# A new order of work on all engines for a linear-attention and gated feed-forward layer

## The chip, the core and the metric

The kernel runs on one core of one Trainium2 chip. The metric is the device time of one execution in microseconds (us). Five engines work side by side, each through its own queue of instructions and in the order of that queue: PE (TensorE, matrix multiplication), DVE (VectorE), ACT (ScalarE), POOL (GpSimd) and SP (SyncE, which here only starts transfers). They wait for one another by semaphores. PE writes into PSUM, which has 8 banks; a matmul group needs a bank that nobody reads any more.

## What is computed

One layer on 2048 tokens of width 448, in bf16: linear attention with softmax features, and a gated feed-forward part, each behind a layer normalisation and with a residual.

```python
q, k, v = split(layernorm(x) @ wqkv)          # 16 heads of 28
pq, pk = q @ w_phi, k @ w_phi                  # per head
phi_q = concat(softmax(pq), softmax(-pq))      # the same for phi_k
kv = einsum("bhsf,bhsd->bhfd", phi_k, v);  z = sum_s phi_k
o = einsum("bhqf,bhfd->bhqd", phi_q, kv) / (einsum("bhqf,bhf->bhq", phi_q, z) + 1e-6)
h = x + o @ wo
y = layernorm(h)
out = h + (sigmoid(y @ w_gate) * (y @ w_up)) @ w_down     # inner width 1792
```

## The kernel before

The tokens are cut into 16 tiles of 128. Keys and values come first: all 16 tiles have to go into `kv` before any output of the attention can be made. The query side follows, and then the feed-forward part in five blocks of 2, 2, 4, 4 and 4 tiles. The query work of the later tiles lies between the matmuls of the first two blocks.

For each tile `t` the query side goes through these tasks:

- `qp`: PE multiplies the normalised tokens with the folded query weights (L516, `Wq,xT`).
- `eqp`, `eqm`: ACT takes the exponentials of plus and minus the result (L653, tile `eq`). The buffer `eq` has 12 places, so tile `t` can be written only when the transpose of tile `t - 12` has read it: tile 13 waits for `eT` 1.
- `hs`: POOL adds halves (L667, `halves`); `sq`: DVE sums (L670); `rq0` on DVE and `rq` on POOL (L674) form the ratio of the two softmax sums.
- `em`: POOL, or DVE by choice, scales the minus half by it (L680, `eq<-eq,rq`).
- `eT`: SP starts a transposing transfer `eqT<-eq` (L688), one tile each for tiles 0 to 3, and two tiles each for 4, 6, 8, 10, 12, 14.
- `num`: PE multiplies with the sums `kvz` (L708, eight matmuls a tile); `rd` and `o` on DVE divide (L716 `rden`, L718 `o_pad`).
- `oT`: a transfer transposes the output of two tiles (L739), and `wo_` (L516, `wo_sb,oT`) projects it.
- `h` adds the residual (L773 on DVE, L759 on ACT for the first tiles); `bst2`, `agg2` (DVE, L776, L778), `ve2`, `pow2`, `nb` (POOL, L779, L781, L792) and `hn` (ACT L794, DVE L796) normalise; `hT` transposes the normalised tokens (for tiles 0 and 1 by PE and a copy, L809 on ACT or L812 on DVE; for the others by a transfer of two tiles, L815, `xT<-hn`).

For each block the feed-forward part runs `gu` on PE (L516, `xT` with `wg_sb` and `wu_sb`, two banks each), `tg` on ACT (L851, tanh), `hh` on DVE (L858), `dn` on PE (L877, `wd_sb,hh`), `fin` on DVE (L884) and `st`, the store (L886). `hh` frees the two banks of its `gu`; `o` frees the bank of its `num`; `fin` that of its `dn`. In the text `gu` 0 is the first of these matmul groups, `num` 10 that of tile 10, and so on. `dm` (L821) are spare matmuls that fill PE's time early in the program and compute nothing.

The order on all engines is written out: `PLAN` (from L30) is a string of task numbers. A suffix `.4-4` names the PSUM banks, and `~` puts a task on its other engine. `planned()` takes the tasks in that order and adds to each what it must wait for (what it reads, and whoever last used its banks); `emit()` then gives every engine its queue:

```python
        for item in PLAN.split():
            if item[-1] == "~":
                t = self.list[int(item[:-1])]
                t.eng, t.fn = t.alt[0], t.alt[2]
```

The durations and landings that stand in the task definitions do not take part in this; they are for whatever makes the string. A transposing transfer gets one of 12 semaphores in turn, a store one of 8.

Of the kernel before, what the change touches and what calls it, by code (L numbers as in the profile page):

```python
# [35 lines left out]
124 123 35 206 210 216 209 36 37 217 686.2-2 687.0-0 688.0-0 689.0-0 690.0-0 684.0-0 691.0-0 692.0-0 693.0-0 150
189.0-2 202 148 207.1-5 190 200 193 38 208 218 211 219 149 212 220 89.3-3 93.4-4 85.6-6 81.2-2 94 82 86 146 196 90
223.0-7 95 144 91 96 92 151 145 147 87 203 83 84 88 221 152 153 39 40 161 159 213 125 126 214 241.1-5 224 234 197.4-4
204 118.6-6 109.2-2 119 154 110 160 155 120~ 157 235 41 242 228 237 225.3-7 111 156 245 246 45 112.6-6 113 115.2-2 116
215 117 114 158 222 226 229 236 227 238 239 46 47 261.1-2 48 162 248 166 163 243.3-6 49 164 262 253 249 170 230  # L40
331.0-7 252 250 265 244 167 165 231 272 255 332 254 259.1-2 232 333 168 334 277.5-6 256 172 247 260 335 257 340
279.0-3 339 169 171 173 263 278 336 174 341 264 337 280 175 271 347.1-7 266 282 338 281 233 342 240 267 251 270 343
283~ 345 268 348 290 284 313.0-2 357 289 295.3-5 176 285 344 273 288 314 356 286 346 296 291 324 297.6-7 325 274 306
50 292 258 275 327 269 307 51 298 318 52 315.2-5 309 317 53 293 308 54 276 328 287 310 299 55 316 320 300 433.0-7 319
311 302 326 294 399.2-3 301 321 303 349 434 322~ 350 382.5-6 443 304~ 400 442 383 435 329~ 402 305 312 323 409 330 358
401 365.1-7 467 468 408 351 359 469.4-4 392 436 474.3-3 470 391 528.2-2 366 360 471 361 362 475 472.4-4 416.0-6 352
368 476 473 364 353 367 385 384 477.3-3 354 529 478~ 355 532.1-1 530 533 369 363 374 550 531 417 551 534 552 375
450.3-5 556 418 553 557 535~ 425 558 554.7-7 451 559 370 555 426 560.1-1 376 482.7-7 419 561~ 479.2-2 460 371 735.0-1
480 483 372 459 728.4-6 484 373 453 737 481 727.5-7 730 452 386 377 485 739 729 733 740 743.2-3 393 731 734 736.0-1 56
387 745 378 738 732 379 752.4-6 380~ 741 767.5-7 747 742 381 754 388 769 748 389 536.0-1 394 757 390 758 776.2-3 395  # L50
771 537 396 772 397 751.4-6 569 778 410 398 562 753 744.1-5 570 781 755 759.0-7 403 756 746 571 782 760.4-6 749 411
761 762 750 427 775.2-3 563 765 768.1-5 763 412 564 766 777 565 764 572 770 573 566 779 496.0-0 773 780 489.7-7 567
493.4-4 774 486.2-2 497 783.1-1 490 487 574 491 575 404 568 428 420 494 576 495 444 786.7-7 421 405 784 406 437 422
488 407 429 445 492 438 498 797.1-2 413 461 806.4-5 799 439 787 499 805.0-3 423 801 414 808 802 790.6-7 811 430
789.1-2 415 431 812 792 446 791 795 798.4-5 440 793 454 796 807 794 800 462 540.1-2 447 803 424 809 804 814.6-7 810
541 455 816 463 599 456 448 441 821.0-3 819 538.4-5 449 600 592 823 539 825 601 820 602 813.1-2 826 457 432 458 577
584 829.6-7 815 822.0-4 603 817 585 831 604 824 818 464 833 830.3-5 578 605 465 837.1-2 834 827 832 593 838.6-7 466
785 835 586 594 839 828 587 595 840 579 836 596 841 514.0-0 843 842 500.4-4 503.3-3 588 844 510.1-1 597 501 507.2-2
589 598 845.6-6 502 580 581 504 606 505 582 583 511 512 590 506 515 517.1-1 846 848.3-3 591 508 509 518 513 521.2-2
849 524.6-6 542.4-7 522 525 516 852.3-5 519 526 543 523 859.0-1 520 614 854 615 868.2-7 857 607 861 858 544.4-6 616  # L60
608 863 867.3-5 864 545 870 527 629 869 622 630 546.0-6 871 623 873 883.1-4 631 874 547 609 624 872 851.2-7 610 632
611 885 612 637 644 633 613 548.0-3 638 634 887 617 888 645 853 618 625 876.5-6 626 855 619 856 892.1-4 627 620~ 549
635~ 628 900.2-7 652 646 659 894 636 621 647 639 653 891.0-3 897 660 788 878 654 661 847 898 655 648 881 662 640 893
902 649 882 663 860.1-4 641 895 875.5-6 642 896 656 643 862 657 905 664 658~ 927.0-3 865 650 866 877 929 665~ 906
936.1-4 931 666 879 932 919.2-7 880 651 938 921 951.5-6 923 924 941 884.0-3 942 953 886 928.1-4 889 955 899.2-7 956
930 890 901 933 935.0-3 920.5-6 934 903 904 960.2-7 943.1-4 962 922 965 937 966 925 945 926 944.2-7 947 939 948
987.5-6 940 959.1-4 946 961 949 952.0-3 950 989 963 954 964 957 967.2-7 991 958 968.1-4 969 970 910.0-0 973 913.3-3
971 911 974 972 981.2-2 907.7-7 908 982 914 983 850 916.1-1 992 917 988.2-3 996.5-6 909 912 990 1003.1-7 1011.0-4 993
994 1005 998 1012.2-3 1001 1007 1002 1013 1008 1014 995.5-6 1017 1015 1016 1018 1027.1-7 997 1036.0-4 999 1000 1029
1038 1031 1004.5-6 1032 1041 1042 1035.2-3 1006 1037 1019.0-4 1009 1020.1-7 1021 1010 1023 1028.5-6 1024 1022 1030  # L70
1025 1053.0-0 1026 1033 1034 1039 1049.4-4 1040 978.1-1 1057.2-2 1046.3-3 1054 1058 1043.5-5 1050 1044 1059 975.5-5
1055 1051 979 1052 980 1045 915 984.1-1 976 1056 1047 1048 1060 977 1061.3-3 985 918 1062 986 1063 1064
"""


# [851 lines left out]
```

## Time and profile before

| | |
|---|---|
| median of three runs | 203.79 us (203.53, 203.79, 204.76) |
| profiled execution, its own time | 203.44 us |
| its span (first to last instruction) | 201.7 us |
| granted TensorE clock | 1.00 |
| PE busy | 195.5 us, 97% |
| DVE, ACT, POOL busy | 134.4, 93.5, 75.7 us |
| longest wait of PE | 2.2 us at L708, for a transpose of query features |

The profile is one execution. Its page gives the busy time of each engine, the chain of waits followed back from the last instruction, and the costliest groups. In a list of waits, `PE ps L708 <- DMA eqT<-eq: 2.2, 1, 2.2` says that PE, before the instruction of line 708, waited for a transfer from `eq` to `eqT`, 2.2 us in total, once, 2.2 at the longest. In a timeline a row has its start, its length, the engine, the line, the operation and the tiles, and how many instructions are joined in it (x4).

### The profile page before, as it was taken

How to read it: one execution, taken by the hardware profiler on the slowest of the kernel's cores; microseconds unless marked ns; L12 is line 12 of the kernel's file. 1: busy time of each engine (PE TensorE's matmuls, PEld its weight loads, DVE VectorE, ACT ScalarE, POOL GpSimd, SP SyncE). 2: the span in 40 equal slices, each digit the busy share in tenths (PEclk: the TensorE clock that was granted, in tenths of full speed). 3: DMA queues.
4: the chain of work that ended last, by engine and by line, in shares of the span. 5: the costliest groups of instructions: out<-in, count | busy, mean ns of one | idle time of the engine just before them, and what ended most of it. 6: DMA issues, size and time to landing. Idle time of an engine off the chain costs nothing.

```text
span 201.7 us, 4990 instructions
## 1 busy us (share of the span) xinstructions
PE 195.5 (97%) x2051; PEld 109.6 (54%) x2051; DVE 134.4 (67%) x315; ACT 93.5 (46%) x179; POOL 75.7 (38%) x130
## 2 busy tenths in 40 slices
PE   8999999999989999978999999999999999999995
PEld 5655545555488858864544444444445444445553
DVE  3999999998899997994779866345411425432052
ACT  2977999999974424263022455424420015330000
POOL 6339799956676789771003560000000000000000
PEclk9999999999999999999999999999999999999999
DMA  5899981699828628599422062200000110000024
GB/s 138 211 248 219 213 297 38 112 395 365 136 54 128 130 55 183 101 163 215 97 52 52 4 149 54 57 0 3 0 0 2 50 44 0 3 0 0 3 79 126
DMA packets 49543, 21.06 MB, mean 104 GB/s; under 512 B 40304, under 2 KB 48496, under 8 KB 49520
## 3 DMA queue, kind: packets, MB, share of 16 engines
q1 hardware_dynamic: 49376, 20.71, 43.8%
q8 instruction: 16, 0.26, 0.6%
q14 instruction: 7, 0.06, 0.1%
q10 hardware_dynamic: 144, 0.03, 0.1%
HBM read 9.20 MB, written 1.84 MB: 55 GB/s over the span
## 4 chain that ended last, share of the span: by engine, by line
PE 90%; DVE 4%; DMA 3%; POOL 1%; issue 1%; ACT 0%; SPq 0%
PE ps L516 57%; PE ps L877 21%; DMA eqT<-eq 3%; PE ps L631 2%; PE ps L821 2%; PE ps L708 2%; PE ps L427 1%; PE ps L445 1%; PE ps L477 1%; PE ps L587 1%; DVE x_sb L773 1%; POOL rs L781 1%; DVE sq L670 1%; DVE hn L788 0%; PE ps L753 0%
## 5 line engine op out<-in xcount | busy, mean ns | idle before, releaser
L516 PE MATMUL ps<-xT,wg_sb 64*128 64x512 bf16 (+1 forms) x490 | 87.6, 333 | 0.6 <-DVE rden L716 0.6
L516 PE MATMUL ps<-xT,wu_sb 64*128 64x512 bf16 (+1 forms) x490 | 87.6, 333 | 0.0
L851 ACT ACTIVATE tg<-ps 128x512 f32<-128x512 f32 (+1 forms) x70 | 34.2, 512 | 75.4 <-PE ps L516 70.1
L858 DVE SCALAR_TENSOR_TENSOR hh<-tg,ps 128x512 bf16<-128x512 f32 (+1 forms) x70 | 39.0, 573 | 30.5 <-ACT tg L851 29.1
L516 PEld LDWEIGHTS ps<-xT,wg_sb 64*128 64x128 bf16 x490 | 45.5, 94 | 21.9 <-issue 1.4
L516 PEld LDWEIGHTS ps<-xT,wu_sb 64*128 64x128 bf16 x490 | 45.5, 94 | 15.4
L877 PE MATMUL ps<-wd_sb,hh 128*128 128x448 bf16 (+2 forms) x252 | 43.3, 332 | 0.0
L877 PEld LDWEIGHTS ps<-wd_sb,hh 128*128 128x128 bf16 x252 | 23.0, 98 | 19.3 <-issue 0.8
L884 DVE SCALAR_TENSOR_TENSOR x_sb<-ps,x_sb 128x448 bf16<-128x448 f32 (+2 forms) x18 | 9.5, 562 | 26.4 <-PE ps L877 26.3
L653 ACT ACTIVATE eq<-ps,rs 128x448 bf16<-128x448 f32 x32 | 18.2, 731 | 0.0
L667 POOL TENSOR_TENSOR halves<-eq 128x448 f32<-128x448 bf16 x14 | 13.4, 971 | 5.7 <-DVE eqT L621 3.3
L680 POOL TENSOR_TENSOR eq<-eq,rq 128x448 bf16<-128x448 bf16 x15 | 14.0, 940 | 0.6
L516 PE MATMUL ps<-Wq,xT 64*128 64x448 bf16 x112 | 12.5, 350 | 0.0
L516 PE MATMUL ps<-Wvc,xT 64*128 64x448 bf16 x112 | 12.4, 350 | 0.0
L516 PE MATMUL ps<-wo_sb,oT 64*128 64x448 bf16 x98 | 11.7, 349 | 0.0
L779 POOL TENSOR_SCALAR rs<-mv 128x1 f32<-128x1 f32 x14 | 2.7, 191 | 23.1 <-DVE mv L778 22.3
L794 ACT ACTIVATE hn<-x_sb,nb,rs 128x512 bf16<-128x512 bf16 x10 | 7.9, 808 | 6.9 <-POOL nb L792 6.9
L516 PE MATMUL ps<-Wk,xT 64*128 64x448 bf16 x98 | 10.7, 350 | 0.0
L601 ACT ACTIVATE hh<-ps,rs 128x448 bf16<-128x448 f32 x16 | 9.6, 677 | 0.4 <-PE ps L587 0.3
L601 ACT ACTIVATE eqT<-ps,rs 128x448 bf16<-128x448 f32 x16 | 9.8, 686 | 0.0
L718 DVE TENSOR_TENSOR o_pad<-ps,rden 128x448 bf16<-128x448 f32 x16 | 9.4, 608 | 0.2
L535 DVE BATCH_NORM_STATS2 st<-x_sb 128x6 f32<-128x448 bf16 x16 | 9.4, 599 | 0.0
(118 smaller groups left out, 219.8 us busy)
## 6 DMA issues: line engine op xcount, KB each, us to landing
wg_sb<-in_B_w_gate_dram SPq DMA_DIRECT2D x2, 896.0 KB, 7.0
wu_sb<-in_B_w_up_dram SPq DMA_DIRECT2D x2, 896.0 KB, 7.9
out_dram<-x_sb SPq DMA_DIRECT2D x14, 112.0 KB, 1.8
x_sb<-in_A_x_dram SPq DMA_DIRECT2D x3, 448.0 KB, 4.5
wd_sb<-in_B_w_down_dram SPq DMA_DIRECT2D x3, 448.0 KB, 11.8
hh<-in_A_wqkv_dram SPq DMA_DIRECT2D x4, 196.0 KB, 3.6
wo_sb<-in_A_wo_dram SPq DMA_DIRECT2D x2, 336.0 KB, 4.4
hh<-in_A_wqkv_dram SPq DMA_DIRECT2D x2, 224.0 KB, 3.4
```

Source lines behind the costliest of these rows:

```text
L516: r = e.matmul(ap(), lhsT=st(blk, rows), rhs=mv(blk, rows), start=first and i == 0, stop=not first and i == 2, tile_position=(rows.start, 0))
L535: task(("bst", t), "dve", 0.53, lambda e, t=t: e.bn_stats(st1[:, t % 4, :], X(t)), [x_ld[t], opt(("agg", t - 4))])
L601: task((key, t), "act", 0.53, lambda e, t=t, s=s, i=i, b=kb: e.activation(signs(ek[s])[:, :, :, i, :], heads2(bank[b()][:, 0:D]), ACT.Exp, ...
L653: task((key, t), "act", 0.53, lambda e, w=w, t=t, i=i, b=bk[j]: e.activation(signs4(eq[:, w, :, 0:GP])[:, :, :, i, :], heads2(bank[b()][:, ...
L667: task(("hs", t), "pool", 0.9, lambda e, w=w, half_=half_, by4=by4: e.tensor_tensor(half_, by4(eq[:, w, :, 0:GP])[:, :, :, 0:DH // 2], by4 ...
L680: return e.tensor_tensor(ap, ap, rq[:, w, :].rearrange("p (k h) -> p k h", h=2)[:, :, :, None].to_broadcast([P, NPAIR, 2, DH]), ALU.mult)
L718: task(("o", t), "dve", 0.56, lambda e, t=t, res=res: e.tensor_tensor(o_pad[:, t % 4, 64 * (t % 2):64 * (t % 2) + D].rearrange("p (h d) -> ...
L794: task(("hn", t), "act", 0.56, lambda e, t=t, hnv=hnv: e.activation(hnv(), windows(X(t)), ACT.Identity, bias=nb[:, t:t + 1], scale=rs2[:, ...
L851: task(("tg", c, f_), "act", 0.51 if n == 4 else 0.3, lambda e, j=j, N=N, b=gb[i]: e.activation(tg[:, j % NSG, 0:N], bank[b()][:, 0:N], AC ...
L858: e.scalar_tensor_tensor(hhT[c % 2][:, f_, 0:N], tg[:, j % NSG, 0:N], 1.0, bank[b()][:, 0:N], op0=ALU.add, op1=ALU.mult), deps)
L877: r = e.matmul(bank[b][:, cols], lhsT=hhT[c % 2][:, f_, ts], rhs=wd_sb[:, f_, cols], start=(f_ == 0), stop=(f_ == FT - 1))
L884: e.scalar_tensor_tensor(X(t)[:, cols], bank[got(first)[0]][:, cols], 0.5, X(t)[:, cols], op0=ALU.mult, op1=ALU.add), [nm, ("hn", t)])
```

## The change

Only the string `PLAN` differs: the order of the tasks on all engines, their banks, and which tasks run on their other engine. It was searched with longer planned landings for the transposes `eT`, `oT` and `hT`. No task, shape or buffer is changed. There are 28 filler matmuls instead of 27. `em` 5 goes from DVE to POOL, the residual `h` 1 and the copy `hT` 1 from DVE to ACT, `hT` 0 from ACT to DVE, and `hn` 4 and `hn` 5 from ACT to DVE.

```diff
 PLAN = """
-18 0 20 16 21 57.7-7 42 22 7 1 58 13 59 8 60 9 6 4 680.0-0 44 14 23 5 24 15 10 25 61 26 11 62 19 12 17 667.0-0 73.0-0
...
+13 10 0 16 18 11 17 21 57.7-7 42 5 3 9 19 4 6 43 20 14 58 2 22 59 7 1 12 15 23 8 60 24 25 61 26 27 28 29 62 667.0-0
...
 """
```

POOL, in the stretch in which the query features of tiles 8 to 15 are scaled; `halves` is `hs`, `rq` is `rq`, `eq<-eq,rq` is `em`. Before, the tiles are in this order: `rq` 9, `hs` 15, `rq` 10, `em` 9, `rq` 11, `em` 11, `rq` 12, `hs` 14, `rq` 13, `em` 10, 13, 12.

```order
L674 TENSOR_TENSOR rq<-rq,sq 128x16
L667 TENSOR_TENSOR halves<-eq 128x448
L674 TENSOR_TENSOR rq<-rq,sq 128x16
L680 TENSOR_TENSOR eq<-eq,rq 128x8x2x28
L674 TENSOR_TENSOR rq<-rq,sq 128x16
L680 TENSOR_TENSOR eq<-eq,rq 128x8x2x28
L674 TENSOR_TENSOR rq<-rq,sq 128x16
L667 TENSOR_TENSOR halves<-eq 128x448
L674 TENSOR_TENSOR rq<-rq,sq 128x16
L680 TENSOR_TENSOR eq<-eq,rq 128x8x2x28 x3
L779 TENSOR_SCALAR rs<-mv 128x1
```

After, the same stretch: `rq` 13, `hs` 14, `rq` 12, `em` 13, `hs` 15, `em` 12, `rq` 15, 10, 14, 11, `em` 10, 11, 15, 14.

```order
L674 TENSOR_TENSOR rq<-rq,sq 128x16
L667 TENSOR_TENSOR halves<-eq 128x448
L674 TENSOR_TENSOR rq<-rq,sq 128x16
L680 TENSOR_TENSOR eq<-eq,rq 128x8x2x28
L667 TENSOR_TENSOR halves<-eq 128x448
L680 TENSOR_TENSOR eq<-eq,rq 128x8x2x28
L674 TENSOR_TENSOR rq<-rq,sq 128x16 x4
L680 TENSOR_TENSOR eq<-eq,rq 128x8x2x28 x4
L779 TENSOR_SCALAR rs<-mv 128x1 x2
```

`em` 13 and 12 moved ahead of `em` 10 and 11. SP's queue has `eT` 8, 12, 10, 14 in this order in both.

PE at the end of the second block. Before, `num` 12, 8, 9, 11, 10, then `dn` 2, `num` 13, `dn` 3, `num` 14, 15, and the output projection `wo_` of tile 4:

```order
L708 MATMUL ps<-kvz,eqT 128x58 x40
L877 MATMUL ps<-wd_sb,hh 128x448 x14
L708 MATMUL ps<-kvz,eqT 128x58 x8
L877 MATMUL ps<-wd_sb,hh 128x448 x14
L708 MATMUL ps<-kvz,eqT 128x58 x16
L516 MATMUL ps<-wo_sb,oT 128x448 x8
L516 MATMUL ps<-xT,wg_sb 128x512
```

After, `num` 10, 13, 12, 9, 11, 8, then `dn` 3 and `dn` 2, `num` 15, 14, and the first `gu` of the third block:

```order
L708 MATMUL ps<-kvz,eqT 128x58 x48
L877 MATMUL ps<-wd_sb,hh 128x448 x28
L708 MATMUL ps<-kvz,eqT 128x58 x16
L516 MATMUL ps<-xT,wg_sb 128x512
L516 MATMUL ps<-xT,wu_sb 128x512
```

All six `num` moved ahead of both `dn`, and a `gu` pair ahead of `wo_`.

SP around the first transposes of query features, before (`eT` 0 and 1, then the second halves of the gate and up weights):

```order
L359 DMA wg_sb<-in_B_w_gate_dram 128x2x1792
L688 DMA_TRANSPOSE eqT<-eq 128x8x128 x2
L359 DMA wu_sb<-in_B_w_up_dram 128x2x1792
L359 DMA wg_sb<-in_B_w_gate_dram 128x2x1792
L359 DMA wu_sb<-in_B_w_up_dram 128x2x1792
```

After:

```order
L359 DMA wg_sb<-in_B_w_gate_dram 128x2x1792
L359 DMA wu_sb<-in_B_w_up_dram 128x2x1792
L688 DMA_TRANSPOSE eqT<-eq 128x8x128
L359 DMA wg_sb<-in_B_w_gate_dram 128x2x1792
L359 DMA wu_sb<-in_B_w_up_dram 128x2x1792
L688 DMA_TRANSPOSE eqT<-eq 128x8x128
```

One weight load moved ahead of `eT` 0, and the two after it ahead of `eT` 1.

More of the change, by code (lines that the diff above doesn't have):

```diff
@@ L36 @@
[L36 to L65, printed above, removed]
@@ new lines @@
+497 495 437 498 407 438 499 446 784 447 454 422 439 797.0-7 415 790.1-3 787 799 440 448 792 801 798.4-5 795 802
+806.2-6 461 796 789.0-7 455 808 441 456 791 462 811 793 449 463 812 464 540.1-3 800 429 423 794 541 457 430 424 803
+805.0-7 599 821.2-6 592 431 807 823 804 809 538.1-3 600 825 465 432 593 829.4-5 458 826 539 810 814.2-6 594 601 584
+595 813.0-7 602 596 577 816 831 466 603 597 585 819 815 820 830.1-3 817 586 822.2-6 833 587 818 604 598 832 578
+837.0-7 835 834 824 838.4-5 827 579 839 605 580 828 836 606 785 840 581 841 507.2-2 517.1-1 582 843 842 514.3-3 588
```

47 lines of the change are left out of this document (36 added, 11 removed).

## The prediction

> **What bounds the kernel now.** I read the page first, then the waits of the matmul engine, then the chain, then the timelines around the one long wait. The page:
>
> ```profile
> span 201.7 us, 4990 instructions
> PE 195.5 (97%) x2051; PEld 109.6 (54%) x2051; DVE 134.4 (67%) x315; ACT 93.5 (46%) x179; POOL 75.7 (38%) x130
> PE 90%; DVE 4%; DMA 3%; POOL 1%; issue 1%; ACT 0%; SPq 0%
> PEclk9999999999999999999999999999999999999999
> ```
>
> PE is busy 195.5 of 201.7 us at full granted clock, and 90% of the chain is PE's own work. The change takes no matmul of the computation away, so all it can win is PE's idle time, 6.2 us, and at most what is filler. The waits that PE shows, engine first, then what was waited for, total, times, longest:
>
> ```profile
> PE ps L708 <- DMA eqT<-eq: 2.2, 1, 2.2
> PE ps L516 <- DVE rden L716: 0.6, 1, 0.6
> ```
>
> One wait matters: 2.2 us, once, for a transpose of query features (`eT`, L688) ahead of `num` (L708). The 0.6 comes at 56 us, at the first feed-forward matmul. The chain through the long wait (start, duration, work):
>
> ```profile
> 84.31 0.36 SPq L688
> 84.72 6.86 DMA eqT<-eq
> 91.58 0.14 issue
> 91.72 0.61 PE ps L708 x16
> 92.33 2.65 PE ps L877 x14
> ```
>
> The transpose issued at 84.72 landed 6.86 us later, and PE had run dry before it:
>
> ```profile
> 88.71 0.85 PE L708 MATMUL ps<-kvz,eqT 112*128 112x58 bf16 x24
> 91.72 0.61 PE L708 MATMUL ps<-kvz,eqT 112*128 112x58 bf16 x16 [2.15 <-DMA eqT<-eq]
> 94.82 0.39 PE L708 MATMUL ps<-kvz,eqT 112*128 112x58 bf16 x8
> 98.25 0.93 PE L516 MATMUL ps<-wo_sb,oT 64*128 64x448 bf16 x8
> ```
>
> Three `num` (8, 9, 12; eight matmuls each) run at 88.71, and `num` 11 and 10 start at 91.72. From there to the end PE hardly waits: it is busy 51.00 of 51.00 and 31.00 of 31.00 us in the next stretches, so what is won here reaches the end.
>
> ```profile
> 99.00:150.00 51.00, 51.00 (x470) 23.26 (x467) 29.70 (x58) 19.35 (x33) 7.81 (x24) 1.00 0.16 37
> 150.00:181.00 31.00, 31.00 (x248) 14.57 (x247) 11.76 (x19) 6.67 (x12) 0.00 (x0) 1.00 0.05 16
> ```
>
> (Columns: window, length, PE, PEld, DVE, ACT, POOL busy, clock, DMA share, GB/s.)
>
> **Why that transpose was late, and what the change moves.** SP's queue holds `eT` 8, 12, 10, 14 in this order in both kernels, each for two tiles. What fed them is on POOL and SP:
>
> ```profile
> 69.75 0.50 POOL L792 TENSOR_SCALAR nb<-mv,rs 128x1 f32<-128x1 f32 x2
> 71.36 1.90 POOL L667 TENSOR_TENSOR halves<-eq 128x448 f32<-128x448 bf16 x2 [1.10 <-DVE sq L670]
> 77.51 0.22 POOL L674 TENSOR_TENSOR rq<-rq,sq 128x16 f32<-128x16 f32 x1
> 77.81 0.94 POOL L680 TENSOR_TENSOR eq<-eq,rq 128x448 bf16<-128x448 bf16 x1
> 80.00 2.74 POOL L680 TENSOR_TENSOR eq<-eq,rq 128x448 bf16<-128x448 bf16 x3
> 82.77 1.90 SPq L688 DMA_TRANSPOSE eqT<-eq  x1
> 84.72 6.24 SPq L688 DMA_TRANSPOSE eqT<-eq  x2
> ```
>
> POOL scales tile 11 at 77.81 (`em`, L680), then 10, 13, 12 in the three from 80.00 to 82.74. So the transposes of 12 and 10 are both released by the last one: 12 issues at 82.77 for 1.90 us, and 10 stands behind it until 84.72, although its data were ready at 80.9 (80.00 and a third of 2.74). The new order puts `em` 13 and 12 ahead of 10 and 11, which suits the queue.
>
> *POOL.* From `hs` 13 to the end of `em` 12 there are now five `hs`, four `rq`, four `em`; then four `rq`, and `em` 10, 11. A `halves` costs 0.93 to 0.97, half of the 1.90 row; an `em` 0.91, a third of 2.74; an `rq` 0.2. That is 5 x 0.95 + 4 x 0.2 + 4 x 0.91 = 9.2 us, and 4 x 0.2 + 2 x 0.91 = 2.6 more. Start: at best 70.25, directly behind the `nb` row, at worst 71.36, if the 1.10 us wait for DVE stays. `em` 12 then ends at 79.4 to 80.6 (82.74 before), `em` 11 at 82.0 to 83.2. I take the early end, since the first `halves` is another tile's now and needs another `sq`.
>
> *The transposes.* `eT` 12 issues at 79.4 and is through SP by 81.3; `eT` 10 issues at 82.0 instead of 84.72. Landing after issue, over all ten (min, median, max):
>
> ```profile
> L688 SPq DMA_TRANSPOSE eqT<-eq x10: 1232/1802/3547, 33.4 to 87.4; - x10
> DMA to landing us min/median/max: 3.1/4.3/6.9
> ```
>
> `eT` 10 so lands at 86.3 by the median and at 88.9 by the maximum; from the late start, 87.5 to 90.1. PE comes to these `num` at about 88.7, as before. The wait of 2.15 goes but for 0.2 at the bad ends; taken: all of it.
>
> *What is late next there.* PE now runs all six `num` (x48) ahead of both down-projections (`dn` 3, `dn` 2, L877). They take 1.4 us, to 90.1 (0.23 each: two `num` start at 91.72, and the next work, of 2.65, starts that much before 94.82, at 92.17). `dn` 3 also needs the last `hh` of the block:
>
> ```profile
> 88.47 1.25 DVE L858 SCALAR_TENSOR_TENSOR hh<-tg,ps 128x256 bf16<-128x256 f32 x3
> 89.64 0.25 DVE L716 RECIPROCAL rden<-ps 128x16 f32<-128x16 f32 x1
> 89.92 0.62 DVE L718 TENSOR_TENSOR o_pad<-ps,rden 128x448 bf16<-128x448 f32 x1
> ```
>
> It ended at 89.72, and in the new order one `rden` (0.25) is put before it: 90.0, beside the 90.1. So `dn` starts at 90.1 with six `num` done, against 92.17 with five done. Gain 92.17 + 0.23 - 90.1 = 2.3. `hn` 5 and 4 come from ACT to DVE behind that, and six divisions of 0.82 follow beside the 5.3 us of the two `dn`; the first of them frees the bank that the next `num` needs, so they are hidden, unless `hn` waits over 4 us for POOL.
>
> *56 us.* `hT` 1 moves from DVE to ACT, and the first matmul pair (L516) can go up to 0.6 earlier. Against this, DVE is the busiest helper afterwards:
>
> ```profile
> 56.50:70.00 13.50, 13.35 (x244) 12.34 (x245) 12.27 (x36) 6.79 (x18) 10.09 (x18) 1.00 0.65 115
> 70.00:89.50 19.50, 19.50 (x276) 14.75 (x274) 17.85 (x48) 7.20 (x17) 15.96 (x30) 1.00 0.65 128
> ```
>
> DVE has 1.2 us to spare in 13.5 and 1.65 in 19.5. `em` 5 leaves it for POOL and `hn` 4, 5 come to it, so the room stays about that. PE reuses a bank pair once DVE's `hh` is through; each `hh` that stands behind a longer instruction can hold PE for one such instruction, 0.3 to 0.6. I take 0.3 gained at 56 us and 0.5 lost in bank waits; bounds +0.6 and -1.5, the latter the room of the second stretch used up nearly once.
>
> *Ends with one answer.* One filler matmul more (28 for 27) lies ahead of 14 us, 0.12 by this row of the chain if it is on the path at all:
>
> ```profile
> 12.77 1.11 PE ps L821 x9
> ```
>  Some stores go later in SP's queue; nothing but the ring waits for them. The last `dn` halves and stores stand in another order, with the same number of columns behind the last matmul: nothing.
>
> Sum: -2.3 - 0.3 + 0.5 = -2.1 us. The profiled execution took 203.44 (span 201.7 and 1.74 around it) and would take 201.3; it lies 0.35 under the median of 203.79, which becomes 201.7.
>
> **Weights ahead of a transpose.** SP's queue now has `wu` 0 before `eT` 0, and `wg` 1 and `wu` 1 between `eT` 0 and `eT` 1.
>
> ```profile
> 33.44 4.32 SPq L688 DMA_TRANSPOSE eqT<-eq  x2
> 43.18 5.43 ACT L653 ACTIVATE eq<-ps,rs 128x448 bf16<-128x448 f32 x10
> 40.00:47.00 7.00, 7.00 (x110) 4.05 (x108) 6.27 (x11) 7.00 (x15) 3.72 (x3) 1.00 1.01 390
> 47.00:56.50 9.50, 8.88 (x100) 4.29 (x96) 8.69 (x25) 9.50 (x20) 6.64 (x11) 1.00 0.85 199
> wu_sb<-in_B_w_up_dram SPq DMA_DIRECT2D x2, 896.0 KB, 7.9
> wd_sb<-in_B_w_down_dram SPq DMA_DIRECT2D x3, 448.0 KB, 11.8
> ```
>
> `eT` 1 can issue at about 36.6: 33.44, half of 4.32, and two loads of 0.5. Its landing, 4.3 later, is 40.9; if it waits for the data of both loads, 1.79 MB at the 390 GB/s of the third row is 4.6 us more, 45.5. Who waits: `eT` 1 frees the buffer into which ACT writes the exponentials of tile 13, fourth in the row of ten from 43.18 on, so at 44.7. ACT is busy 7.00 of 7.00 and 9.50 of 9.50 us: each us it stalls there is passed on, to `hT` 1, which now is ACT's: 20 exponentials of 0.52 (ten take 5.2 to the next one's start) and three casts of 0.4 stand before it from 43.18 on, so ACT could start it at 54.8, and PE had its matmuls ready for it about 1 us later (first matmul 56.56 less the 0.6 of waiting, in the chain and the waits). An `eT` 1 up to 45.7 costs nothing.
> The Trainium skill's page "DMA: Bandwidth & Descriptors", section "Queues, rings and completion order", says that on each DMA engine the descriptors of one issuing queue are consumed in ring order, which speaks for the later landing, 45.5. By it ACT would stall 0.8 us, inside the room of 1 us, and rival C would be 0.2 us away; no row here shows it for a transpose behind weights.
>
> **The rivals.** A, *the wait only moves*, 0.20. For it: `dn` now stands behind all six `num`, so a late `eT` 10 stops everything, and `rden` of `num` 10 stands ahead of the last `hh`. And the first matmuls of the next block need `hT` 4 right behind `num` 14, at about 96.1, with no `wo` pair ahead (98.25 before):
>
> ```profile
> 94.35 1.26 SPq L815 DMA_TRANSPOSE xT<-hn  x1
> xT<-hn SPq DMA_TRANSPOSE x7, 2.8
> ```
>
> Issued at 94.35 as before, it lands 2.8 later, at 97.2, and PE waits 1.1. Against it: POOL is done with `em` earlier. A wait of 0.8 to 1.9 is left: gain 0.2 to 1.3, time 202.5 to 203.6.
>
> B, *DVE sets the pace* from 56 to 89 us, 0.08: the bank waits reach 1.5 or a little more. Time 202.6 to 203.8. Against it: DVE had room, though little.
>
> C, *slower*, 0.08: `eT` 1 lands late. The `wd` loads took 11.8 us to land, `wu` 7.9, and 36.6 + 11.8 is 48.4. Behind the stalled exponentials stand all later ones, `hT` 1 and the first `tg`. From 45.7 on each us is one of PE; at 47.8 the gain of 2.1 is gone, and later it is slower: 48.4 gives 204.4, and with a POOL that is late by it too, because `hs` 13 to 15 need these exponentials, and so the L708 wait back in full, 206.6. For it: ACT without a gap. Against it: the early `wu` 0 uses a quiet stretch of the queue, and the estimate for both loads is 45.5.
>
> D, *more than I count*, 0.09: both ends of 56 us come out well, and no bank waits: 200.7 to 201.2.
>
> E, 0.05, is slower by over 1% at a place that I haven't seen, since hundreds of instructions are moved. That the order does not do what it says has no chance of its own: POOL's and PE's rows show it.
>
> **How the numbers follow.** The main case, 0.50: the L708 wait gone, gain 1.5 to 2.6, time 201.2 to 202.3, likeliest 201.7. 1% of 203.79, about what a measurement of this kernel can tell, is 2.04: faster is below 201.75, slower above 205.83. Faster: somewhat over half of the main case, 0.30, and D, 0.09: 0.39. Slower: E and half of C, 0.09. Same: the rest, 0.52. The range 200.8 to 203.9 holds the main case, A and B and most of D; it leaves out C, E and the lower end of D, 0.16.
>
> **What would show it.** Right: no wait for `eqT` over 0.3 at L708; `em` 12 ends near 79.4, the third two-tile transpose issues near 82; `dn` follows 48 matmuls of L708 at about 90; PE's busy time unchanged, and its idle time down from 6.2 to about 4. Wrong: a wait for `xT` or `hh` at L516 near 96 (A); short waits for `hh` or `rden` between 56 and 89 that sum to over 1 us (B); ACT waiting for `eqT` at L653 near 45, and the first wg matmul later than 56.56 (C).

## The result and the profile after

The new order takes 201.08 us, the median of four runs (200.94 to 201.40). The kernel before, on the same chip, took 203.66 (203.42 to 204.76, four runs). The ratio is 0.986, with a 95% interval of 0.982 to 0.990. The profiled executions took 203.44 before and 201.07 after, 2.37 us apart; their spans are 201.7 and 199.3. One of the four runs of before, 204.76, belongs to an upper group of its times, which is explained further down.

The page of the new kernel: PE's busy time is what it was (195.2 for 195.5), and the chain is PE's at 95% instead of 90%, with no transfer left in it. PE's idle time, the span less its busy time, went from 6.2 to 4.1.

```profile
span 199.3 us, 4989 instructions
PE 195.2 (98%) x2052; PEld 107.0 (54%) x2052; DVE 133.3 (67%) x315; ACT 92.3 (46%) x178; POOL 76.2 (38%) x131
PE 95%; DVE 2%; POOL 1%; issue 0%; ACT 0%
```

What PE waited for, in full. The 2.2 us at L708 are gone, and nothing has come in their place (the 0.8 at the start of the program stood in the kernel before as well):

```profile
PE ps L427 <- PEq L912: 0.8, 1, 0.8
PE ps L516 <- DVE rden L716: 0.5, 1, 0.5
```

POOL, SP and PE around the place, from their timelines:

```profile
77.80 0.94 POOL L680 TENSOR_TENSOR eq<-eq,rq 128x448 bf16<-128x448 bf16 x1
80.13 3.64 POOL L680 TENSOR_TENSOR eq<-eq,rq 128x448 bf16<-128x448 bf16 x4
78.77 3.01 SPq L688 DMA_TRANSPOSE eqT<-eq  x1
82.00 1.83 SPq L688 DMA_TRANSPOSE eqT<-eq  x1
88.63 1.55 PE L708 MATMUL ps<-kvz,eqT 112*128 112x58 bf16 x48
90.01 5.46 PE L877 MATMUL ps<-wd_sb,hh 128*128 128x448 bf16 x28
95.31 0.62 PE L708 MATMUL ps<-kvz,eqT 112*128 112x58 bf16 x16
95.86 0.39 PE L516 MATMUL ps<-xT,wg_sb 64*128 64x512 bf16 x1
```

`em` 12 ends at 78.74 (82.74 before) and `eT` 12 issues at 78.77. `em` 10 and 11 are the first two of the four from 80.13; `eT` 10 issues at 82.00 (84.72 before) and, in the trace, lands at 86.52. PE comes to its `num` at 88.63, as it did before (88.71), and now runs all six, both `dn` and the next block without a gap. From there on the two kernels run in step, the new one about 2.4 us earlier: the stretch of L516 that follows the last `num` of this place begins at 95.93 in the chain, and began at 98.32 before.

So in these two profiles the whole difference stands at one place. What it was there is the question of the experiments.

### The profile page after: what moved, and what is told of

Its sections match the earlier page's. It is cut to its first block, busy times and chain, and to the rows that moved or that the text cites. A ratio compares the mean times of both kernels' runs of the same rounds, so it can differ in the third digit from the quotient of the medians.

```text
span 199.3 us, 4989 instructions
## 1 busy us (share of the span) xinstructions
PE 195.2 (98%) x2052; PEld 107.0 (54%) x2052; DVE 133.3 (67%) x315; ACT 92.3 (46%) x178; POOL 76.2 (38%) x131
## 4 chain that ended last, share of the span: by engine, by line
PE 95%; DVE 2%; POOL 1%; issue 0%; ACT 0%
PE ps L516 63%; PE ps L877 21%; PE ps L631 2%; PE ps L708 2%; PE ps L821 2%; PE ps L427 1%; PE ps L477 1%; PE ps L587 1%; PE ps L445 1%; POOL rs L781 1%; PE ps L493 0%; DVE hn L788 0%; PE ps L753 0%; DVE xT L812 0%; PE ps L726 0%
## 5 line engine op out<-in xcount | busy, mean ns | idle before, releaser
L516 PE MATMUL ps<-xT,wg_sb 64*128 64x512 bf16 (+1 forms) x490 | 88.0, 333 | 0.5 <-DVE rden L716 0.5
L516 PE MATMUL ps<-xT,wu_sb 64*128 64x512 bf16 (+1 forms) x490 | 88.0, 333 | 0.1
L516 PEld LDWEIGHTS ps<-xT,wg_sb 64*128 64x128 bf16 x490 | 45.2, 94 | 23.0 <-issue 1.4
L516 PEld LDWEIGHTS ps<-xT,wu_sb 64*128 64x128 bf16 x490 | 45.2, 94 | 16.2 <-PE ps L516 0.3
L680 POOL TENSOR_TENSOR eq<-eq,rq 128x448 bf16<-128x448 bf16 x16 | 14.9, 944 | 0.2
L516 PE MATMUL ps<-Wvc,xT 64*128 64x448 bf16 x112 | 12.5, 350 | 0.1
L516 PE MATMUL ps<-Wq,xT 64*128 64x448 bf16 x112 | 12.3, 350 | 0.0
L516 PE MATMUL ps<-wo_sb,oT 64*128 64x448 bf16 x98 | 11.6, 349 | 0.0
L516 PE MATMUL ps<-Wk,xT 64*128 64x448 bf16 x98 | 10.6, 350 | 0.0
L781 POOL TENSOR_TENSOR rs<-rs,neghalf 128x1 f32<-128x1 f32 x16 | 8.7, 553 | 1.3 <-DVE rs L779 0.6
L621 POOL TENSOR_TENSOR eqT<-eqT,rsum 128x896 bf16<-128x896 bf16 x5 | 8.5, 1699 | 1.8 <-ACT eqT L601 1.8
```

What stands on the lines that cost most here:

```text
L516: r = e.matmul(ap(), lhsT=st(blk, rows), rhs=mv(blk, rows), start=first and i == 0, stop=not first and i == 2, tile_position=(rows.start, 0))
L621: return e.tensor_tensor(phi[t % NPHI][:, :, 0:GP].rearrange("p k (a d) -> p k a d", d=DH), ek[s].rearrange("p (k a d) -> p k a d", a=4, d ...
L680: return e.tensor_tensor(ap, ap, rq[:, w, :].rearrange("p (k h) -> p k h", h=2)[:, :, :, None].to_broadcast([P, NPAIR, 2, DH]), ALU.mult)
L781: task(("pow2", t), "pool", 0.53, lambda e, t=t: e.tensor_tensor(rs2[:, t:t + 1], rs2[:, t:t + 1], neghalf[:, 0:1], ALU.pow), [("ve2", t), ...
```

## The experiments

My theory (R): the gain is the landing of `eT` 10 against PE's arrival at its `num`, and nothing else in the new order matters for the time. The main rival (W): a new order of hundreds of instructions works as a whole, and a single move of it gives little. The table gives the medians; the runs of before were taken with them on the same chip. The new order itself ran on another occasion (201.08); the lower group of before, described below the table, has its median between 203.38 and 203.57 on all of them, so times may be compared across the rows to about 0.2 us. `num`, `dn` and the other names are those of the kernel's tasks; a filler is one spare matmul (`dm`).

| run | order it starts from, and the edit | median us | range | before there | ratio, 95% |
|---|---|---|---|---|---|
| e1_pool_only | before; POOL: `em` 13, 12 ahead of 11, 10 | 201.41 | 200.98 to 201.85 | 204.63 | 0.986 (0.980 to 0.992) |
| e2_sp_only | before; SP: `eT` 10 ahead of `eT` 12 | 201.15 | 200.72 to 201.27 | 204.63 | 0.984 (0.977 to 0.991) |
| e3_undo_pool | after; POOL: `em` 13, 12 behind 10, 11 | 206.08 | 204.38 to 207.36 | 204.63 | 1.010 (1.006 to 1.014) |
| e4_pe_only | before; PE: `dn` 2 ahead of `num` 11, 10 | 201.68 | 201.47 to 202.26 | 204.63 | 0.988 (0.982 to 0.993) |
| e5_eT1_first | after; SP: `eT` 1 ahead of `wg` 1, `wu` 1 | 201.19 | 201.03 to 201.52 | 203.39 | 0.988 (0.984 to 0.992) |
| e6_eT1_last | after; SP: `eT` 1 behind `wd` 0 to 2 | 206.69 | 205.98 to 207.75 | 203.39 | 1.014 (1.008 to 1.019) |
| e7_undo_pool_fill | e3 with 28 fillers ahead of `num` 10 | 205.37 | 205.20 to 205.57 | 203.39 | 1.008 (1.004 to 1.011) |
| e8_before_fill | before with 20 fillers ahead of `num` 11 | 204.41 | 203.69 to 204.89 | 203.39 | 1.003 (1.000 to 1.006) |
| e9_before_less_fill | before without 9 fillers at 12.8 us | 203.60 | 201.70 to 205.70 | 203.57 | 0.995 (0.991 to 0.999), of its eight runs up to 203.79 |
| e10_after_less_fill | after without 9 fillers of that place | 201.32 | 200.99 to 201.56 | 203.57 | 0.988 (0.983 to 0.993) |

The medians of before differ because its times lie in two groups. Over the three sets and the first four runs, 31 lie at 203.2 to 203.9 and 14 at 204.6 to 205.5. What the groups are is answered below with two more profiles of before (b1 and b2). For e1, e2 and e4 seven of the thirteen runs of before are of the upper group, so their ratios contain some of the distance between the groups; against the lower group's median there, 203.46, they gained 2.05, 2.3 and 1.8 us.

### One move at a time

Each of three runs changes one thing in the order of before. In the strings below 448, 441, 424 and 431 are `em` 13, 12, 10 and 11; 449 and 432 are `eT` 12 and 10; 845, 848 are `dn` 2 and 3; 510, 507, 517 are `num` 11, 10, 13.

```diff
 POOL, e1
-431
...
-424
...
 448
 441
+431
+424
```

> The order of before with one thing changed: on POOL the scalings of tiles 13 and 12 stand ahead of those of 11 and 10, as in the new order; no other engine's queue changes. Theory R (the release of the transposes is the whole gain): eT 12 issues at about 81.0 instead of 82.77, eT 10 at about 82.9 instead of 84.72, and lands at 87.2 to 89.8; PE comes to its num at 89.4, so the wait of 2.2 us at L708 falls to 0 to 0.4. The transpose hT 4 landed at 97.2, which is then 0.2 to 0.4 too late at L516. Time 1.6 to 2.2 us below before, 201.5 to 202.1. Rival W (the gain belongs to the whole new order, its single moves bring little): the wait only moves on, and the time falls by less than 0.7.

```diff
 SP, e2
+432
 449
...
-432
```

> The order of before with one thing changed: SP's queue has eT 10 ahead of eT 12; POOL is left as it was. Theory R: eT 10's data are ready at 80.9, so it issues there and lands at 85.3 to 87.9, ahead of its num. eT 12 issues at 82.9 and lands at 87.2 to 89.8, where its num wants it at 88.7: a wait of 0 to 1.1 in place of 2.2. Time 1.0 to 2.2 us below before. Rival W: less than 0.7. A third view, that the transposes share one pool of transfer engines and the sum of their work decides (rival Q): the wait moves from eT 10 to eT 12 in full, and the time stays within 0.5 of before.

```diff
 PE, e4
+845.6-6
 510.1-1
 507.2-2
-845.6-6
-517.1-1
 848.3-3
+517.1-1
```

> The order of before with one thing changed: on PE dn 2 stands ahead of num 11 and 10, and num 13 behind dn 3, so that 2.65 us of other work lie where PE waited. POOL and SP are left as they were, and eT 10 is as late as before (landing 91.6). Theory R, in its general form (only the landing against PE's arrival counts): PE waits 0.3 for the last hh and nothing for eT 10; 1.5 to 2.0 us below before, 201.8 to 202.3, with 0.2 to 0.5 lost at L516 for hT 4. Rival P (the late eT 10 also delays what follows it: the divisions, the output transposes and eT 14): the wait comes back at num 14, at wo_ or at the first gu of the next block, and the time falls by less than 1.0.

All three give what the new order gives (201.08), or nearly: e2 lies 0.1 above it, e1 0.3 and e4 0.6. Their ratios lie within each other's intervals. e2 swaps two neighbours in one queue, and that is all it takes. SP and PE in the profile of e2:

```profile
80.80 9.54 SPq L688 DMA_TRANSPOSE eqT<-eq  x3
88.54 1.37 PE L708 MATMUL ps<-kvz,eqT 112*128 112x58 bf16 x40
89.75 2.81 PE L877 MATMUL ps<-wd_sb,hh 128*128 128x448 bf16 x14
```

The first of the three transposes issues at 80.80, as soon as `em` 10 is done, and the five `num` run through. In the trace `eT` 10 lands at 85.22 and `eT` 12 at 88.10, both ahead of PE. That answers the view that the transposes' common work decides (Q): with one swap both are in time.

e4 leaves the landing as late as it was (91.27 in the trace) and lets PE do 2.65 us of other work meanwhile:

```profile
88.58 0.85 PE L708 MATMUL ps<-kvz,eqT 112*128 112x58 bf16 x24
89.65 2.82 PE L877 MATMUL ps<-wd_sb,hh 128*128 128x448 bf16 x14 [0.22 <-DVE hh L858]
92.31 0.62 PE L708 MATMUL ps<-kvz,eqT 112*128 112x58 bf16 x16
```

0.22 us of waiting for the last `hh` is left, near the 0.3 expected, and the 0.2 to 0.5 us for `hT` 4 that e1 and e4 were to lose did not show: it landed at 96.3 and 96.8 in these kernels, just ahead of the matmuls that need it (96.51 and 96.96), and was not waited for. Theory R holds in its general form: the landing against PE's arrival. W falls for the gain. That the new order's other moves are without effect is shown at their sum only.

### Undoing it in the new order

```diff
 POOL, e3
-448
...
-441
...
 424
...
 431
+448
+441
```

> The new order with one thing undone: on POOL the scalings of 13 and 12 stand behind those of 10 and 11 again. Theory R: eT 12 is released at about 82.8 instead of 78.8, eT 10 issues at 85 to 86 instead of 82.0 and lands at 89.3 to 92; num 10 is first of the six and wanted at 88.7, so PE waits 0.6 to 3.3 us, and the time is 0.6 to 3.3 us above the new order, 201.7 to 204.4. Rival W: the rest of the new order carries the gain, and the time stays within 0.4 of the new order.

The wait comes back, and the time rises by 5.0 us over the new order, more than the 0.6 to 3.3 that I expected. The wait, 3.1, lies inside those bounds, and the landing, 92.18, 0.2 beyond the latest that I gave; what the forecast didn't have is slow work behind the wait, and 0.6 us by which this execution was late ahead of it. Its timelines of POOL, SP and PE:

```profile
79.94 0.76 POOL L674 TENSOR_TENSOR rq<-rq,sq 128x16 f32<-128x16 f32 x4 [2.43 <-DVE rq L672]
80.66 5.43 POOL L680 TENSOR_TENSOR eq<-eq,rq 128x448 bf16<-128x448 bf16 x6
84.33 8.41 SPq L688 DMA_TRANSPOSE eqT<-eq  x3
92.32 2.48 PE L708 MATMUL ps<-kvz,eqT 112*128 112x58 bf16 x48 [3.08 <-DMA eqT<-eq]
```

POOL idled 2.43 us for a reciprocal from DVE, because in the new order the scalings of 13 and 12 had filled most of that time. So `eT` 12 issued at 84.33, later than before (82.77), and `eT` 10 landed at 92.18. That is the wait of 3.08. But the 48 matmuls of L708 took 2.48 us and not 1.55, and the two `dn` behind them 5.83 and not 5.46. The stretches behind the wait (columns: window, length, busy PE, PEld, DVE, ACT, POOL, granted clock, DMA share, GB/s):

```profile
90.00:92.00 2.00, 0.00 (x0) 0.00 (x0) 0.76 (x3) 0.80 (x3) 0.84 (x3) 0.99 0.84 185
92.00:94.00 2.00, 1.68 (x36) 1.72 (x37) 0.85 (x3) 0.00 (x0) 0.00 (x0) 0.50 0.94 196
94.00:96.00 2.00, 2.00 (x23) 1.28 (x21) 1.66 (x5) 0.00 (x0) 0.00 (x0) 0.66 0.76 189
```

The granted clock fell to 0.50 behind the wait and came back within the last of these stretches (by the trace's record of the clock it was halved from 91.95 to 95.37). Between the two profiles the 5.0 us are: 3.1 of waiting, 1.3 of slower matmuls behind it, and 0.6 that PE was late already when it came to its `num` (89.24 for 88.63). That last part has nothing to do with the edit, which first acts near 76 us: PE was 0.6 behind at the first matmuls of L516 already (10.96 us for 10.34).

### Keeping PE busy through the wait

e7 is e3 with spare matmuls of L821 (128x256, constants by constants) in front of `num` 10; e8 is the same idea in the order of before. Both move no other instruction. Their lines are numbered two higher.

```diff
 PE, e7
+28 fillers in bank 2
 507.2-2
 PE, e8
+20 fillers in bank 1
 510.1-1
```

> The kernel with POOL's scalings put back (new order, 13 and 12 behind 10 and 11), and 28 spare filler matmuls ahead of num 10, about 3.0 us of PE work that computes nothing, in the bank of num 10. That kernel waited 3.1 us at L708, and its granted clock was 0.50 and 0.66 in the 4 us behind the wait. Clock theory: PE's idleness itself took the clock down, so that with PE kept busy the clock stays at 1.00, the 48 matmuls of L708 take 1.5 us and not 2.5, the first dn not 3.0 but 2.65 each, and the time is 1.0 to 2.0 us below that kernel, 204.1 to 205.1, though the transpose lands no sooner. Rival (the fillers only fill a wait; the slow stretch comes from the transfers or from something else): the same time, 205.6 to 206.6, or more.

> The order of before with 20 spare filler matmuls, 2.1 us that compute nothing, ahead of num 11, where PE waited 2.2 us for eT 10. The times of before lie in two groups, 203.2 to 203.7 and 204.6 to 205.3. Clock theory: the upper group are executions in which the wait took the clock down for a few us; with the wait filled only the lower group is left, median 203.3 to 203.7, and no run above 204.3. Rival (the groups have another cause): two groups again, a third or more of the runs above 204.5.

In e7 the clock stayed up:

```profile
89.93 3.31 PE L823 MATMUL ps<-const-bfloat16-1.0 128*128 128x256 bf16 x28 [0.83 <-DVE hh L860]
93.08 1.52 PE L710 MATMUL ps<-kvz,eqT 112*128 112x58 bf16 x48
```

The 48 matmuls take 1.52 us again, and the clock in all stretches from 88 to 96 us is 1.00. The time is 205.37 against 206.08, and its runs lie within 0.4 us where those of e3 lie over 3. The fillers themselves came late: they waited 0.83 for a bank and ended at 93.08, past the landing (92.05 in the trace), so they ate about 1 us of what the clock gave back. The gain of 0.7 is below the 1.0 to 2.0 that I expected. That idleness takes the clock down is shown by the rows, and by all runs: each one's mean granted clock is on record, and it is 1.00 in the six runs of e7 and below 1.00 (0.992 or 0.983) in nine of the ten of e3. The tenth, at 1.00, is e3's fastest, 204.38.

e8 missed its forecast of the time (203.3 to 203.7): its runs lie at 203.69 to 204.89, between the two groups and over both edges. What it says of the clock stands all the same: all ten runs have a mean clock of 1.00, where before has less in 13 of 41. In its profile a new wait of 1.0 us stands at L518, for a residual addition on DVE. That stood behind a division, and the division had waited 1.56 us for an output transpose (landed 4.8 us after its issue, 2.75 in before). Its cause is told below.

### The two groups of times of the kernel before

> The kernel before, unchanged, for another profile. Its times lie in two groups, 203.2 to 203.9 and 204.6 to 205.5. If this execution is of the upper group: by the clock theory PE's wait at L708 is 2.2 or longer and the granted clock behind it is below 1.00 for some us; by the rival, that the transpose is later still, the wait is 3.5 to 4.0 with the clock at 1.00 throughout. If it is of the lower group it should repeat the first profile: a wait of 2.1 to 2.4.

> The same once more, for the other group if the first look shows only one: the wait at L708, the landing of eT 10, the packet of the instruction queue beside it, and the granted clock behind the wait.

The two profiled executions took 203.26 and 204.83 us, one of each group. Their waits are the same, 2.10 and 2.11 us. The first (b1), behind the wait:

```profile
91.53 0.61 PE L708 MATMUL ps<-kvz,eqT 112*128 112x58 bf16 x16 [2.10 <-DMA eqT<-eq]
91.98 2.81 PE L877 MATMUL ps<-wd_sb,hh 128*128 128x448 bf16 x14
```

The second (b2):

```profile
91.37 0.61 PE L708 MATMUL ps<-kvz,eqT 112*128 112x58 bf16 x16 [2.11 <-DMA eqT<-eq]
91.83 4.50 PE L877 MATMUL ps<-wd_sb,hh 128*128 128x448 bf16 x14
```

Its stretches from 92 us on:

```profile
92.00:94.00 2.00, 2.00 (x9) 0.86 (x8) 0.85 (x3) 0.87 (x2) 0.00 (x0) 0.67 1.00 243
94.00:96.00 2.00, 2.00 (x7) 0.89 (x6) 0.00 (x0) 0.00 (x0) 0.00 (x0) 0.50 0.98 223
```

The same wait, and behind it a `dn` of 4.50 us for 2.81, at a clock of 0.67 and 0.50. The difference, 1.69, is about the distance of the two (204.83 - 203.26 = 1.57). So the wait of before cost 2.1 us always and some 1.6 more in a part of the executions. Each run's mean clock bears this out: of the 41 runs of before that have it on record, it is 0.992 in all 13 of the upper group and 1.00 in all 28 of the lower.

Why only in a part? The Trainium skill's page "TensorE: Matmul & The Clock Gate", section "Part 1: The HAM clock gate (the "warmup" mystery)", says that the clock is halved after an idle window of about 3.4 us, and that the window runs freely, not from the kernel's start, so that where in it the work falls decides when the clock changes. The traces' records of the clock show such a grid. The clock was halved for 3.41 us in b2 and in e3 and for 6.83, twice that, in e6 (below), and the stretches of full clock between two changes are 85.33, 88.75 and 44.37 us long, or 25, 26 and 13 times 3.413. In b2 the change at 92.67 puts a window at 89.26 to 92.67, which holds the whole wait (89.26 to 91.37). In the other two profiles of before the grid, counted on from its first change at 4.28 and 5.02, cuts the wait: at 89.61 in b1, which leaves at most 1.92 us of it in one window, and at 90.35 in the first profile, which leaves 1.37. In e3 the window up to 91.95 holds 2.71. So 2.11 and 2.71 us of idleness in one window halved the clock, and 1.92 and 1.37 did not; these are four executions. Where the page asks for an idle window, a window idle for 2.11 of its 3.41 us was enough here, and the measurement decides.

The 24 runs of the kernels without the wait (after, e1, e2, e4, e5, e10) lie between 200.7 and 202.3, with no second group.

### The weights ahead of `eT` 1

```diff
 SP, e5
+eT 1
 wg 1
 wu 1
-eT 1
 SP, e6
-eT 1
 wd 0
 wd 1
 wd 2
+eT 1
```

> The new order with one thing undone: on SP eT 1 issues ahead of wg 1 and wu 1 again. In the new order it landed at 44.79 us, 1.67 behind wu 1, and ACT's exponential of tile 13 started at 44.81, so ACT did not stall. Theory: eT 1 lands at about 40 to 42, nobody is sooner for it; the time stays within 0.3 of the new order, 200.8 to 201.4. Rival (the new order lost something to the late eT 1 that the waits don't show): 0.3 to 1.0 faster than the new order.

> The new order with more of one thing: on SP eT 1 issues behind wd 0, 1 and 2 as well, 1.34 MB more. Ring theory (a transpose starts once the loads ahead of it in SP's queue have moved their data): wd 2 landed at 50.2 in the new order, so eT 1 lands at 48.5 to 51.5 and ACT waits 3.7 to 6.7 us for it at L653; of this the first 1.0 costs nothing, as the prediction had it, and PE loses 2.7 to 5.7: 203.8 to 206.8. Rival (transposes pass the loads): eT 1 lands at issue plus 3 to 5, about 46, ACT waits 1 to 2 us, and the time rises by at most 1.0.

In the trace of the new order `eT` 1 issues at 36.59 and lands at 44.79; `wu` 1, ahead of it in the queue, lands at 43.12. In e5 it issues at 36.87, with no load in between, and lands at 39.94. In e6 it lands at 49.99, 0.75 behind `wd` 2. With loads in between it landed behind the last of them, both times. The transfer packets of the new order show why: those of the transpose, told by their size of 256 bytes, begin at 42.16 us and none of them earlier, though it was issued at 36.59, when nearly all packets of the two loads (3584 bytes each, the last at 42.58) have begun. That agrees with the rule of the Trainium skill's page "DMA: Bandwidth & Descriptors", section "Queues, rings and completion order": descriptors of one queue are consumed in ring order.

For the time e5 is the new order (201.19 and 201.08), so the late `eT` 1 costs nothing there. But the margin was nil: ACT's exponential of tile 13 started at 44.81, 0.02 us behind the landing, and within 0.03 us of the pace that it keeps in e5, where the data had long been there. e6 shows what lies beyond it. What ACT and PE wait for:

```profile
ACT eq L653 <- DMA eqT<-eq: 4.8, 1, 4.8
PE ps L516 <- ACT eq L653: 4.0, 1, 4.0
```

The stretches, with the columns as above:

```profile
47.00:51.00 4.00, 0.23 (x8) 0.11 (x4) 1.37 (x3) 0.98 (x2) 1.62 (x2) 0.91 0.24 40
51.00:54.00 3.00, 2.77 (x25) 1.38 (x25) 0.56 (x3) 3.00 (x7) 0.11 (x1) 0.50 0.00 0
54.00:57.00 3.00, 3.00 (x22) 1.09 (x19) 1.69 (x5) 2.41 (x6) 2.21 (x4) 0.50 0.23 45
```

ACT stalls 4.8 us, PE 4.0 of them, and the clock is halved for 6.8 us behind (50.27 to 57.10 by its record). The median is 5.6 us over the new order, inside the 2.7 to 5.7 expected, but that is in part luck: the forecast counted the wait alone. In the profiled execution, 207.75 and so 6.7 over that of the new order, the wait is 4.0 of it and the halved clock most of the rest. The four runs fall in two pairs like those of before: 207.07 and 207.75 with a mean clock of 0.983, 205.98 and 206.31 with 0.992. And the stall itself is not all the loads' doing: a packet of the instruction queue, of which the next part tells, began at 47.15 us in the middle of this `eT` 1.

### Why the landing took 6.9 us

`eT` 10 of before needed 6.86 us from issue to landing; the other transposes of two tiles mostly 4.3 to 5. In the ten traces of before, the new order and e1 to e8 I set the landing of each transpose of two tiles from 57 us on beside the 16 KB packets of the instruction queue (the page lists them as a queue of its own, 16 packets, 0.26 MB). They come about every 250 instructions of PE (254 on average in before).

```
transposes, issue to landing, us                        min   median  max   count
eT (16 blocks of 128x128), no packet begun on the way   4.25  4.39    4.55    14
eT, a packet begun on the way                           4.30  4.84    6.86    46
oT and hT (8 blocks), no packet begun on the way        2.71  2.74    3.90   129
oT and hT, a packet begun on the way                    2.75  2.98    4.99    11
```

Most packets lie near a transpose's start or its end, where they cost little. The five longest two-tile landings (5.88 to 6.86) are all `eT` 10, in kernels where a packet falls 2.7 to 4.8 us into it: before, e3, e4, e7 and e8. In before it starts at 89.55. The stretch from there, and those beside it:

```profile
88.20:89.60 1.40, 1.36 (x36) 1.03 (x30) 1.29 (x5) 0.66 (x2) 1.23 (x4) 1.00 1.22 189
89.60:91.00 1.40, 0.00 (x0) 0.00 (x0) 1.33 (x5) 0.81 (x1) 1.13 (x5) 1.00 1.35 28
91.00:92.40 1.40, 0.68 (x18) 0.62 (x19) 0.63 (x2) 0.76 (x2) 0.51 (x2) 1.00 1.03 233
```

For 1.4 us the transfer engines are busy (share 1.35; a packet's whole time counts where it begins, so that the share can pass 1) and the packets that begin hold 28 GB/s, where they held 189 and 233. The table alone doesn't settle it: in before the packet begins 4.83 us into `eT` 10, later than a transpose of the first row takes in all. This `eT` 10 was slow for another reason too, which stays open; e9 below measures what is left without the packet. The output transpose that e8 waited for met such a packet too: the 20 fillers are 40 instructions, and the packet that lay at 99.71 in before came at 97.75, 1.15 us into it.

e9 takes nine fillers from the start of before, which has nothing to do with the transposes, to move the packet. e10 does the same in the new order, as a control.

```diff
 PE, e9
-nine dm of L821 between the last kp 1 and the first vp 0
 PE, e10
-nine dm of L821 between the last kp 1 and the first vp 1
```

> The order of before without the nine filler matmuls at 12.8 to 13.9 us; nothing else is touched, and POOL, SP and the transposes stand as before. In the traces the two-tile transposes land 4.3 to 4.6 us after their issue, and up to 6.9 where a 16 KB packet of the instruction queue starts in the middle of them; in before such a packet starts at 89.55, while eT 10 is on its way. Fetch theory: these packets come at fixed places in PE's instructions, about every 256 of them; with 18 instructions fewer ahead of it the packet of 89.55 comes behind the wait for eT 10, which then lands at 89.4 to 90.0 and not at 91.6; the wait of 2.2 falls to 0 to 0.6, and the time by 1.4 to 2.2 us. Rival (eT 10 is late because of its issue at 84.72 alone): the wait and the time stay within 0.4 of before.

> The control for that: the new order without nine fillers of the same place. eT 10 landed at 86.5 there, 2.2 us ahead of PE. Both theories: the time stays within 0.3 of the new order, 200.8 to 201.4, since the fillers stand in PE's idle time; if the fillers themselves cost or bring something, it shows here.

In e9's profiled execution, of 201.7 us, the packet begins at 89.99 and `eT` 10, issued at 84.83, lands at 89.86, 5.04 us after its issue and just ahead of the packet. The last row here is the stretch behind it, with the columns as above:

```profile
84.83 2.59 SPq L688 DMA_TRANSPOSE eqT<-eq  x1
88.81 0.85 PE L708 MATMUL ps<-kvz,eqT 112*128 112x58 bf16 x24
90.00 0.61 PE L708 MATMUL ps<-kvz,eqT 112*128 112x58 bf16 x16 [0.33 <-DVE rden L716]
90.00:91.40 1.40, 1.40 (x22) 0.94 (x22) 1.34 (x4) 0.81 (x1) 1.18 (x4) 1.00 1.76 64
```

The issue is as late as before, and the wait is 0.33 instead of 2.2. (The row names a reciprocal, for which this `num` does not wait; the landing is 0.14 us ahead of the start, as it is in before, 91.58 to 91.72.) The slow stretch has moved with the packet: 64 GB/s, now behind the landing. So in this execution the late issue alone was not the whole cause: with it, `eT` 10 was only just late, and the packet of before made some 1.8 us of that (a landing of 6.86 us for 5.04).

By its median, 203.60, however, e9 is where before is (203.57), as the rival had forecast, and the profiled execution is the fastest of its ten. They lie from 201.70 to 205.70: four at 201.7 to 202.2, four at 203.6 to 203.8, and two above 204.9, these two with a mean clock of 0.992 and the other eight at 1.00. With 0.13 us between landing and packet a race is likely, lost in some executions, of which some then lost the clock as well; that is argued, since only one of them has a trace. The control, e10, stays at 201.32, and the fewer fillers by themselves bring nothing. In it the packets fell elsewhere too: one begins 3.95 us into `eT` 12, which landed after 5.98, without being waited for.

## Why the prediction was right, point by point

- **The bound and the place.** Right: 2.2 us at L708, and what is won there reaches the end. The later stretches run in step. PE's idle time was to fall to about 4 and fell to 4.1.
- **POOL.** `em` 12 was to end at 79.4 and did at 78.74; `em` 11 at 82.0, and by half of the row from 80.13 it was 81.95. That the second figure fits is luck. `hs` 13 started at 68.81, 1.4 us ahead of the early start that I chose, since the `nb` before it ended that much sooner; and POOL then waited twice for DVE, 0.73 and 0.67 us, where my sum has no wait:

```profile
72.82 0.97 POOL L667 TENSOR_TENSOR halves<-eq 128x448 f32<-128x448 bf16 x1 [0.73 <-DVE sq L670]
79.41 0.77 POOL L674 TENSOR_TENSOR rq<-rq,sq 128x16 f32<-128x16 f32 x4 [0.67 <-DVE rq L672]
```

- **The transposes.** `eT` 10 was to issue at 82.0 and did at 82.00; landing 86.3 by the median, measured 86.52. The bound of 6.9 that I took from the longest row was a landing with an instruction packet in it; without one, in e9, it took 5.04.
- **What is late next.** `dn` was to start at 90.1 and started at 90.01. Gain there 2.3, measured 92.17 + 0.23 - 90.01 = 2.39.
- **56 us and DVE.** These terms were mis-sized, though their sum was small: +0.3 and -0.5, together 0.2 lost. In this pair of profiles the first pair of L516 starts at 56.34 (56.56 before), 0.22 gained, and PE is at `num` at 88.63 (88.71), so 0.14 of that was lost on the way. Other profiles take the first part back: with the new order up to there the pair starts at 56.62 (e5), 56.62 (e10), 56.79 (e7) and 56.92 (e3), and with the old one at 56.22 to 56.67 in eight. The start of the program alone moves it by more than 0.3, and no gain at 56 us is shown. The loss on the way is the steadier figure: 32.13 to 32.21 us from the pair to `num` in the old order, 32.25 to 32.29 in the new (after, e5, e10), about 0.1. It is not the bank waits that I had forecast: PE's longest gap there is the one before 58.54, 0.06 us. The same 210 matmuls of L516 take 12.20 in the chain before (the first row), and 12.39 and that gap now (the other two):

```profile
56.56 12.20 PE ps L516 x210
56.34 2.15 PE ps L516 x36
58.54 10.24 PE ps L516 x174
```

- **The sum.** 2.1 predicted, 2.37 between the profiles. The medians are 2.58 apart, since one of the four runs of before is of its upper group; the prediction did not know the 1.6 us that the wait cost there, though one of its three times, 204.76, lay apart. By its number, 201.08, the result lies below the main case (201.2 to 202.3) and in the span of rival D; of D's two conditions one came, no bank waits, and the other, both ends of 56 us, is not shown.
- **Rival A** did not come: `hT` 4 issued at 90.72 and landed at 93.44, and L516 followed `num` at 95.86 without a wait. The 94.35 that I had kept from before was wrong by 3.6 us: among other things `hT` 4 now stands ahead of `oT` 8 in SP's queue. **B** did not come either; PE's list of waits has none between 57 us and the end. **C** was nearer than its chance said: the landing that I gave as 45.5 was 44.79, and the time at which ACT wanted it, given as 44.7, was 44.81. Its mechanism is shown by e6, with two corrections: the stall passes to PE through a bank of `qp` (0.8 us of room, not 1.0 through `hT` 1), and the clock adds to it.
- **The ring order** that I weighed decided for the later landing, 45.5, and rightly so: 44.79 was measured, with the packets in that order.

## What to carry to other kernels

A long wait for a transfer is first asked whether the queue that issues it holds something ahead of it that is not ready yet: here a swap of two neighbours in SP's queue, or four scalings in another order on POOL, or other work of PE in the place of the wait each gave nearly all that a new order of everything gave (201.15, 201.41 and 201.68 us for 201.08). A wait of some 2 us on TensorE can cost more than its length, because it can halve the clock behind it (2.1 us of waiting, 1.6 more behind it); where a kernel's times lie in two groups, the granted clock behind its longest wait is the row to read. And a transfer whose landing decides needs a margin for an instruction packet in its way, which cost some 1.8 us here.

## What the runs showed of the hardware that I had not expected

- The granted clock fell to 0.50 behind a wait of 2.1 us in one execution and stayed at 1.00 behind the same wait in another; the price was 1.6 us. Behind 3.1 us (e3) and 4.0 us (e6) it fell as well, and with spare matmuls in the wait (e7, e8) it did not in any of 16 runs. The halved stretches lasted 3.41 us or twice that, and whether the wait of 2.1 us fell into one window of that grid went with whether the clock fell.
- A 16 KB packet of the instruction queue in the middle of a transposing transfer goes with a stretch of 1.4 us at 28 GB/s instead of about 200, and with a landing after 6.86 us that took 5.04 where the packet came behind it (e9). The packets follow PE's own instruction count, so that in one profile nine matmuls less at 13 us moved one of them at 90 us past a landing.
- A transpose issued behind weight loads in the same queue landed 1.7 and 0.75 us after the last of them, 8.2 and 10.5 us after its own issue (the new order and e6), for 3.1 with no load in between (e5).
